# Listing the copies of a finished value product one slot later, behind an exponential, in a bucketed attention with a gated FFN

## The chip, the core and the metric

The kernel runs on one core of a Trainium2 chip. The engines of the core are TensorE (PE in the profile, with its weight loads apart as PEld), VectorE (DVE), ScalarE (ACT), GpSimd (POOL) and SyncE (SP, which only issues transfers here). Each engine takes its own list of instructions in order; an instruction waits on semaphores for what it needs of other engines. The metric is the device time of one execution in microseconds, lower being better.

## The reference

The first half is attention in which a query sees only the keys of its own hash bucket: six signs of a projection of q and of k make the bucket, and scores of other buckets are masked.

```python
mask = q_bucket[:, :, :, None] == k_bucket[:, :, None, :]
scores = scale * np.matmul(q, k.transpose(0, 1, 3, 2))
scores = np.where(mask, scores, -1000000000.0)
scores = scores - np.max(scores, axis=-1, keepdims=True)
attn = np.exp(scores)
attn = attn / (np.sum(attn, axis=-1, keepdims=True) + 1e-09)
x = np.matmul(attn, v)
```

The heads' outputs are then set side by side (512 channels) and go through a gated FFN: a causal convolution with 5 taps over the sequence gives a gate, sigmoid of it is multiplied with `x @ w_val`, and the product goes through `w_out`. Batch 4, 8 heads, sequence 768, head size 64, all in fp32.

## The kernel before

A **unit** is one head of one batch (32 units, numbered from 0). Its 768 queries are cut into 6 **tiles** of 128, so there are 192 tiles. One pass of the main loop (line 541) is a **slot**: slot k writes down, for several tiles at once, the steps at different stages. The order in which the Python code writes them down is the order of each engine's list (`manual_schedule`, line 522); no planner moves them.

In slot k the list is, in this order:

- ACT copies the transposed probabilities of tile k-4 out of PSUM (`keep_transposed`, line 369, two copies). With the last tile of a unit, the unit's value product is put into the list `avs`.
- DVE takes the row maxima of tile k (line 317), then the scale and the bias of its exponential (lines 323 and 327). In even slots the row sums and reciprocals of two earlier tiles stand between (lines 341 and 346).
- POOL multiplies tile k-2 by its reciprocals (`normalise`, line 351).
- PE makes the scores of tile k+1 (line 311, four matmuls). They go into one of two PSUM buffers named s, so tile k+1 reuses the buffer of tile k-1.
- ACT makes the exponential of tile k (line 335), which reads the scores and the bias.
- `convs` is stepped (line 569), in odd slots only while k is under 60 and in every slot from 60 on. A step of `pair_x` first splits the pair's outputs into a high part (two casts on DVE, line 403) and a low part (two subtractions on POOL, line 404), and in later steps makes the convolution's five taps (lines 412 and 414).
- `moes`, the FFN's matmuls of the batch before, is stepped: four matmuls a step (lines 445 and 470), with their products and splits on DVE and POOL (lines 450, 454 and 456) and the output copies (lines 476 and 478). In some slots no step, in a few three.
- preparation of the next unit, and other small lists.
- in odd slots `avs` is stepped twice (lines 583 and 584). One step of `attn_v` is two matmuls into the PSUM tile av, one for each half of the queries; six steps make a unit's value product.
- PE transposes tile k-3 (line 360, six transposes into two PSUM buffers named tp).

A unit's last tile comes to `keep_transposed` in a slot with k mod 6 = 3. The value product's six steps stand in the slots with k mod 6 = 3, 5 and 1. In the kernel before, the sixth step, at the end of the slot with k mod 6 = 1, also writes down what follows the matmuls: for the first unit of a pair (an even unit) the memset of a new tile x on POOL (line 387), then two copies of av into x on ACT (line 391), and for the second unit of a pair (an odd unit) the entry of `pair_x` into `convs` (line 395). PSUM tile av has one buffer, so the next unit's value product needs these copies done.

Of the kernel before, what the change touches and what calls it, by code (L numbers as in the profile page):

```python
# [26 lines left out]
def kernel(  # L27
# [109 lines left out]
    def load_conv():  # L137
        if conv_w.dtype == mybir.dt.int64:
            w = const.tile([P, NP * KW, 2], I32, name="cw64")
            nc.sync.dma_start(out=w, in_=conv_w.bitcast(I32).rearrange("p (n t) -> p n t", t=2))  # L140
            t = const.tile([P, NP * KW], FP32, name="cwt")
            yield
            a, d = yield from from_float64(w, t)
            yield
            nc.vector.tensor_tensor(out=cw_sb, in0=d, in1=a, op=ALU.add)
        else:
            nc.sync.dma_start(out=cw_sb, in_=conv_w)

    def load_weights():
        parts = [(src[:, c, :], hl[0][:, c, :], hl[1][:, c, :])  # L150
                 for src, hl in ((w_val, wv), (w_out, wo)) for c in range(NP)]
        here = []

        def fetch():
            if len(here) == len(parts):
                return
            src = parts[len(here)][0]
            if src.dtype == mybir.dt.int64:
                w = wst.tile([P, 512, 2], I32, name="w64")
                nc.sync.dma_start(out=w, in_=src.bitcast(I32).rearrange("p (n t) -> p n t", t=2))  # L160
            else:
                w = wst.tile([P, 512], FP32, name="w32")
                nc.sync.dma_start(out=w, in_=src)
            here.append(w)

        fetch()
        for n, (_, hi, lo) in enumerate(parts):
            yield
            yield from split_weight(here[n], hi, lo, fetch)

    def load_raw(i):
        if i < len(units):
            b, h = units[i]
            raws[i] = raw.tile([P, S], FP32, name="r")
            nc.sync.dma_start(out=raws[i], in_=qk[b, h])

    def load_values(i):
        b, h = units[i]
        if h % 2 == 0:
            vts[i] = vp.tile([P, KB, P], FP32, name="vt")  # L180
            nc.sync.dma_start(out=vts[i], in_=v[b, h // 2])
        else:
            vts[i] = vts[i - 1]
# [145 lines left out]
    def exponentials(k):  # L329
        s, nb = ss.pop(k), nbs.pop(k)  # L330
        p = pp.tile([P, 2, HS], FP32, name="p")
        if k % 2 == 0:
            cur["sm"] = small.tile([P, 2, 2], FP32, name="sm")
        sm = cur["sm"]
        nc.scalar.activation(out=p, in_=s[:, :, 0:HS], func=AF.Exp, bias=nb, scale=gs.pop(k), accum_out=sm[:, k % 2, 0:1])  # L335
        ps[k] = (p.rearrange("p a b -> p (a b)"), sm)
# [12 lines left out]
    def normalise(k):  # L349
        p, _ = ps[k]  # L350
        nc.gpsimd.tensor_scalar(out=p, in0=p, scalar1=rcs.pop(k), scalar2=1.0, op0=ALU.mult, op1=ALU.mult)  # L351
# [22 lines left out]
    def attn_v(i, pts):  # L374
        b, h = units[i]
        hh, c = h % 2, h // 2
        av = ps_v.tile([P, 512], FP32, name="av")
        vt = vts[i]
        for kb in range(KB):
            if kb:  # L380
                yield
            for s, pt in enumerate(pts):
                nc.tensor.matmul(out=av[s * D:(s + 1) * D, 0:HS], lhsT=vt[:, kb, hh * D:(hh + 1) * D], rhs=pt[kb // 3][:, kb % 3, :],  # L383
                                 start=(kb == 0), stop=(kb == KB - 1), tile_position=(0, s * D))
        if hh == 0:
            x = cur["x"] = xp.tile([P, S + KW - 1], FP32, name="x")
            nc.gpsimd.memset(x[:, 0:KW - 1], 0.0)
        x = cur["x"]
        for s in range(2):
            o = KW - 1 + s * HS  # L390
            nc.scalar.copy(out=x[hh * D:(hh + 1) * D, o:o + HS], in_=av[s * D:(s + 1) * D, 0:HS])  # L391
        if hh == 1:
            if c == 0:
                cur["xs"], cur["g"] = {}, []
            convs.append(pair_x(b, c, x, cur["g"], cur["xs"]))

    def pair_x(b, c, x, gs, xs_):
        for o in (0, HS):
            xh = xs.tile([P, HS], FP32R, name="xh")
            xl = xs.tile([P, HS], FP32R, name="xl")  # L400
            xs_[(c, o)] = (xh, xl)
            x0 = x[:, KW - 1 + o:KW - 1 + o + HS]
            nc.vector.tensor_copy(out=xh, in_=x0)  # L403
            nc.gpsimd.tensor_tensor(out=xl, in0=x0, in1=xh.bitcast(FP32), op=ALU.subtract)  # L404
        yield
        g = gp.tile([P, S], FP32, name="g")
        gs.append(g)
        for k in range(KW):
            yield
            w = cw_sb[:, c * KW + k:c * KW + k + 1]  # L410
            if k == 0:
                nc.gpsimd.tensor_scalar(out=g, in0=x[:, 0:S], scalar1=w, scalar2=1.0, op0=ALU.mult, op1=ALU.mult)  # L412
            else:
                nc.vector.scalar_tensor_tensor(out=g, in0=x[:, k:k + S], scalar=w, in1=g, op0=ALU.mult, op1=ALU.add)  # L414
        if c == NP - 1:
            yield
            for g in gs:
                nc.scalar.activation(out=g, in_=g, func=AF.Sigmoid)
            cur["gates"] = 2
            moes.append(moe(b, xs_, gs))  # L420
# [84 lines left out]
    avs, convs, moes, us = [], [], [], {}  # L505
    accs = [(ps_m, "m")]

    def step(gens):

        while gens:  # L510
            try:
                return next(gens[0])
            except StopIteration:
                gens.pop(0)
# [7 lines left out]
    with tc.manual_schedule(engines=ENGINES):  # L522
        for i in range(5):
            load_raw(i)
        load_values(0)
        rest = first_prep()
        next(rest)
        weights = [[load_weights()], [load_conv()]]
        preps = [first_bits(), prep(1)]
        scores(0)  # L530
        next(preps[1])
        step(preps)
        step(weights[0])
        step(weights[1])
        ahead = [early_bits()]
        near = {i: [bits(i)] for i in (4, 8, 12)}
        marks = {10: near[4], 11: ahead, 16: near[4], 17: ahead, 22: ahead, 28: ahead, 34: near[8], 40: near[8], 46: ahead, 52: ahead,
                 54: ahead, 56: ahead, 58: near[12], 60: near[12], 62: ahead, 64: ahead}
        for gens in near.values():
            step(gens)  # L540
        for k in range(N + LAG + 1):
            if 0 <= k - LAG - 1:
                keep_transposed(k - LAG - 1)
            pair = k % 2 == 0 and 0 <= k - 2 < N
            if k < N:
                maxima(k)
            if pair:
                row_sums(k - 2)
            if k < N:
                factors(k)  # L550
            if pair:
                recip(k - 2)
            if 0 <= k - 2 < N:
                normalise(k - 2)
            if k < N:
                shifts(k)
            if k == 0:
                finish([rest])
            if k + 1 < N:
                if tiles[k + 1][0] != tiles[k][0]:  # L560
                    finish(preps)
                    preps = [prep(tiles[k + 1][0] + 1)]
                scores(k + 1)
            if k < N:
                exponentials(k)
            if k - 1 in marks and k - 1 not in (11, 17):
                step(marks[k - 1])
            if k >= 60 or k % 2:
                step(convs)

            thin = k // 6 % 8 in (7, 0) and k < 186
            for _ in range(3 if cur["gates"] else (1, 0)[k % 2] if thin else 1):
                step(moes)
            cur["gates"] = max(0, cur["gates"] - 1)
            step(preps)
            if k in marks:
                step(marks[k])
            if k in (3, 7, 9, 13, 15):
                step(weights[1])
            if k % 6 != 3 and k > 4:  # L580
                step(weights[0])
            if k % 2:
                step(avs)
                step(avs)
            if 0 <= k - LAG < N:
                transposes(k - LAG)
        accs[:] = [(ps_m, "m"), (ps_t, "tp"), (ps_s, "s"), (ps_t, "tp"), (ps_s, "s")]
        finish(avs)
        cur["gates"] = 0
        cur["end"] = True  # L590
        while convs:
            step(convs)
            step(moes)
        finish(moes)
# [59 lines left out]
```

## Time and profile before

| what | us |
|---|---|
| median of 3 runs | 614.88 |
| lowest and highest | 613.47, 615.2 |
| the profiled execution, its own time | 613.79 |
| span of the profiled execution | 611.9 |
| TensorE busy | 585.5 |
| VectorE busy | 428.8 |
| ScalarE busy | 420.2 |
| GpSimd busy | 386.5 |

The span is the stretch of the profiled execution from the first instruction to the last. Busy time is the union of an engine's instructions. A row of instructions in order of time gives start and length in us, engine, line, operation, output and inputs, and in brackets the time that the engine stood idle before it with what ended that idle time. A row of a group gives the total of its busy time, the mean length in ns, and the idle time before it. In the chain of waits each piece is the work that the next piece waited for. TensorE's instructions are pipelined, so neighbouring rows can overlap by some hundredths to tenths of a microsecond.

### The profile page before, as it was taken

Reading aid. Unit: us, or ns where it says so; the run is one execution under the profiler, and the core shown is the slowest. Engines: PE = TensorE matmul, PEld = TensorE weight load, DVE = VectorE, ACT = ScalarE, POOL = GpSimd, SP = SyncE. Lnnn points to the kernel's source line nnn. Section 1 sums busy time; section 2 is a strip of 40 time slices with the busy share of each in tenths; the row PEclk is TensorE's granted clock in tenths of the full one; section 3 lists DMA queues with packets and bytes.
Section 4 is the critical chain, followed back from the end, with each engine's and each line's share of the span. In section 5 each row is a group of like instructions: output and inputs, shape, how many; then the busy total and the mean of one; then the engine's idle time right before and its main releaser. Section 6 shows DMA issues by size and latency. Waiting matters only on the chain.

```text
span 611.9 us, 10670 instructions
## 1 busy us (share of the span) xinstructions
PE 585.5 (96%) x3496; PEld 422.1 (69%) x3496; DVE 428.8 (70%) x1020; ACT 420.2 (69%) x881; POOL 386.5 (63%) x373
## 2 busy tenths in 40 slices
PE   5889999999999999999999999999999999999997
PEld 2656665665567777776667777777768787775995
DVE  6788889898776856587657857578765867565532
ACT  2778888787787766677796767677787676764300
POOL 3566877878656766677655768477745776454321
PEclk9999999999999999999999999999999999999999
DMA  7476566455742342233334323423333123100111
GB/s 231 123 206 198 161 175 177 131 160 148 226 109 81 83 121 70 82 105 86 111 90 123 80 74 89 113 83 92 101 87 90 45 55 100 47 19 1 51 52 51
DMA packets 29030, 64.64 MB, mean 106 GB/s; under 512 B 4936, under 2 KB 10056, under 8 KB 28976
## 3 DMA queue, kind: packets, MB, share of 16 engines
q1 hardware_dynamic: 28832, 63.93, 38.1%
q8 instruction: 28, 0.46, 0.3%
q14 instruction: 26, 0.21, 0.1%
q10 hardware_dynamic: 144, 0.03, 0.0%
HBM read 30.60 MB, written 7.86 MB: 63 GB/s over the span
## 4 chain that ended last, share of the span: by engine, by line
PE 80%; ACT 15%; DVE 3%; issue 1%; DMA 1%; ACTq 0%; DVEq 0%
PE av L383 22%; PE s L311 20%; PE tp L360 16%; PE m L470 8%; PE m L445 7%; ACT p L335 6%; ACT pt L369 5%; ACT x L391 3%; PE m L217 2%; PE tp L445 1%; PE tp L470 1%; PE s L470 1%; PE s L445 1%; DVE nm L317 1%; DMA packed<-in_proj_dram 1%
## 5 line engine op out<-in xcount | busy, mean ns | idle before, releaser
L351 POOL TENSOR_SCALAR p<-p,ri 128x768 f32<-128x768 f32 x192 | 205.4, 1074 | 152.1 <-DVE nb L327 130.9
L317 DVE TENSOR_REDUCE nm<-s 128x1 f32<-128x768 f32 x192 | 182.8, 952 | 72.1 <-PE s L311 71.3
L369 ACT COPY pt<-tp 128x384 f32<-128x384 f32 x384 | 165.9, 485 | 86.0 <-PE tp L360 85.3
L335 ACT ACTIVATE p<-s,nb,gs 128x768 f32<-128x768 f32 x192 | 193.0, 1005 | 29.6 <-DVE nb L327 26.9
L360 PEld LDWEIGHTS tp<-ident,p 128*128 128x128 f32 x1152 | 129.5, 142 | 75.4 <-issue 50.1
L360 PE MATMUL tp<-ident,p 128*128 128x128 f32 x1152 | 164.7, 279 | 2.6 <-ACT pt L369 1.6
L383 PE MATMUL av<-pt,vt 128*64 128x384 f32 x768 | 144.9, 498 | 0.0
L311 PE MATMUL s<-ak,aq 76*128 76x384 f32 x384 | 117.9, 388 | 14.6 <-ACT p L335 12.6
L311 PE MATMUL s<-bk,bq 128*128 128x384 f32 x384 | 101.7, 346 | 0.3 <-DVE bq L285 0.3
L383 PEld LDWEIGHTS av<-pt,vt 128*64 128x64 f32 x768 | 47.0, 136 | 60.5 <-issue 60.4
L311 PEld LDWEIGHTS s<-ak,aq 76*128 76x128 f32 x384 | 59.2, 194 | 28.8 <-ACT p L335 25.2
L414 DVE SCALAR_TENSOR_TENSOR g<-x,cw_sb,g 128x768 f32<-128x768 f32 x64 | 75.9, 1187 | 2.2 <-POOL g L412 2.1
L311 PEld LDWEIGHTS s<-bk,bq 128*128 128x128 f32 x384 | 71.5, 193 | 1.1 <-DVE bq L285 0.8
L456 POOL TENSOR_TENSOR hl<-ht,hh 128x384 fp32r<-128x384 f32 x32 | 32.3, 1009 | 40.0 <-DVE hh L454 40.0
L200 POOL TENSOR_TENSOR bq<-r,aq 128x768 fp32r<-128x768 f32 x31 | 56.8, 1833 | 0.1
L391 ACT COPY x<-av 64x384 f32<-64x384 f32 x64 | 30.4, 475 | 32.1 <-PE av L383 31.5
L404 POOL TENSOR_TENSOR xl<-x,xh 128x384 fp32r<-128x384 f32 x32 | 33.4, 1057 | 17.0 <-DVE xh L403 17.0
L327 DVE TENSOR_SCALAR nb<-nm,gs 128x1 f32<-128x1 f32 x192 | 40.6, 211 | 3.5
L445 PE MATMUL m<-xh,wv 128*128 128x384 f32 x200 | 42.8, 338 | 0.0
L450 DVE TENSOR_TENSOR ht<-m,g 128x384 f32<-128x384 f32 x25 | 13.9, 556 | 37.9 <-PE m L445 33.4
L335 ACT ACTIVATION_READ_ACCUMULATOR p<-s,nb,gs 128x1 f32 x192 | 39.5, 206 | 0.0
L470 PE MATMUL m<-wo,hh 128*128 128x512 f32 x144 | 38.1, 394 | 0.0
(86 smaller groups left out, 477.9 us busy)
## 6 DMA issues: line engine op xcount, KB each, us to landing
r<-in_qk_dram SPq DMA_DIRECT2D x32, 384.0 KB
vt<-in_v_dram SPq DMA_DIRECT2D x16, 384.0 KB
out_dram<-o SPq DMA_DIRECT2D x24, 256.0 KB
ak<-aq SPq DMA_DIRECT2D x31, 192.0 KB
bk<-aq SPq DMA_DIRECT2D x31, 192.0 KB
bk<-bq SPq DMA_DIRECT2D x31, 192.0 KB
bq<-aq SPq DMA_DIRECT2D x31, 192.0 KB
hh<-in_qk_dram SPq DMA_DIRECT2D x16, 192.0 KB
```

The costliest lines, as they stand in the source:

```text
L200: nc.gpsimd.tensor_tensor(out=bq, in0=r, in1=aq.bitcast(FP32), op=ALU.subtract)
L311: nc.tensor.matmul(out=s[:, hf, 0:HS], lhsT=lq[0:n, qs], rhs=rk[0:n, hf * HS:(hf + 1) * HS], start=n == M, stop=n == P)
L317: nc.vector.tensor_reduce(out=nm, in_=s[:, :, 0:HS], axis=AX.XY, op=ALU.max, negate=True)
L335: nc.scalar.activation(out=p, in_=s[:, :, 0:HS], func=AF.Exp, bias=nb, scale=gs.pop(k), accum_out=sm[:, k % 2, 0:1])
L351: nc.gpsimd.tensor_scalar(out=p, in0=p, scalar1=rcs.pop(k), scalar2=1.0, op0=ALU.mult, op1=ALU.mult)
L360: nc.tensor.transpose(out=tp[:, n * P:(n + 1) * P], in_=p[:, kb * P:(kb + 1) * P], identity=ident)
L369: nc.scalar.copy(out=pt[:, :, qo:qo + P], in_=tp[:, 0:HS].rearrange("p (a b) -> p a b", b=P))
L383: nc.tensor.matmul(out=av[s * D:(s + 1) * D, 0:HS], lhsT=vt[:, kb, hh * D:(hh + 1) * D], rhs=pt[kb // 3][:, kb % 3, :], start=(kb == 0), s ...
L391: nc.scalar.copy(out=x[hh * D:(hh + 1) * D, o:o + HS], in_=av[s * D:(s + 1) * D, 0:HS])
L414: nc.vector.scalar_tensor_tensor(out=g, in0=x[:, k:k + S], scalar=w, in1=g, op0=ALU.mult, op1=ALU.add)
L445: nc.tensor.matmul(out=acc[:, 0:HS], lhsT=wv[wi][:, c, j * P:(j + 1) * P], rhs=xs_[(c, o)][xi], start=(m == 0), stop=(m == 11))
L470: nc.tensor.matmul(out=acc, lhsT=hs[(o, j)][hi][:, tb * P:(tb + 1) * P], rhs=wo[wi][:, j, :], start=(m == 0), stop=(m == 11))
```

## The change

A `yield` is put between the value product's last matmuls and what follows them, so the sixth step ends with the matmuls. In the slots with k mod 6 = 2 one more step of `avs` is written down, directly behind that slot's exponential and ahead of the step of `convs`; it holds the memset, the two copies and the entry into `convs`. Since the entry is made in the slot with k mod 6 = 2 ahead of the step of `convs`, from slot 60 on the first step of `pair_x` stays in that slot, where it is in the kernel before. On ACT the two copies of line 391 now stand behind the two transposed copies of tile k-4 and the exponential of tile k of that slot, instead of ahead of them.

```diff
@@ attn_v
             for s, pt in enumerate(pts):
                 nc.tensor.matmul(out=av[s * D:(s + 1) * D, 0:HS], lhsT=vt[:, kb, hh * D:(hh + 1) * D], rhs=pt[kb // 3][:, kb % 3, :],
                                  start=(kb == 0), stop=(kb == KB - 1), tile_position=(0, s * D))
+        yield
         if hh == 0:
             x = cur["x"] = xp.tile([P, S + KW - 1], FP32, name="x")
             nc.gpsimd.memset(x[:, 0:KW - 1], 0.0)
@@ the main loop
             if k < N:
                 exponentials(k)
+            if k % 6 == 2:
+                step(avs)
             if k - 1 in marks and k - 1 not in (11, 17):
                 step(marks[k - 1])
             if k >= 60 or k % 2:
                 step(convs)
```

## The prediction

> **What bounds the kernel now.** I read the page first, then the waits, the chain in a thin early stretch, and then the instructions in order of time around the copies.
>
> ```profile
> span 611.9 us, 10670 instructions
> PE 585.5 (96%) x3496; PEld 422.1 (69%) x3496; DVE 428.8 (70%) x1020; ACT 420.2 (69%) x881; POOL 386.5 (63%) x373
> PE 80%; ACT 15%; DVE 3%; issue 1%; DMA 1%; ACTq 0%; DVEq 0%
> ...
> L335 ACT ACTIVATE p<-s,nb,gs 128x768 f32<-128x768 f32 x192 | 193.0, 1005 | 29.6 <-DVE nb L327 26.9 <-DVE cw L97 0.8 <-POOL p L351 0.6
> ...
> L391 ACT COPY x<-av 64x384 f32<-64x384 f32 x64 | 30.4, 475 | 32.1 <-PE av L383 31.5
> ...
> PE s L311 <- ACT p L335: 12.6, 31, 1.5
> ```
>
> TensorE (PE) is busy 96% of the span and carries 80% of the chain: it sets the end, and a change counts only where it moves a stall of PE. Its largest one is line 311 (scores) waiting for line 335 (exponential): 12.6 us in 31 waits. The two score buffers explain it: the scores of tile n+2 need the buffer that the exponential of tile n has read. The copies of line 391 keep ScalarE (ACT) busy 30.4 us, and ACT stands idle 31.5 us before them because they are listed right behind the value matmuls that they read.
>
> I write c for the slot with c mod 6 = 1 in which a unit's value product ends, and t for the time from the start of its first copy today. Here is unit 4 (instructions in order of time, then a piece of the chain; columns: start, length, what).
>
> ```profile
> 107.83 0.44 PE L360 MATMUL tp<-ident,p 128*128 128x128 f32 x2
> ...
> 107.94 0.96 ACT L391 COPY x<-av 64x384 f32<-64x384 f32 x2 [0.74 <-PE av L383]
> 108.93 0.86 ACT L369 COPY pt<-tp 128x384 f32<-128x384 f32 x2
> 109.67 1.01 ACT L335 ACTIVATE p<-s,nb,gs 128x768 f32<-128x768 f32 x1
> ...
> 110.83 0.98 PE s L311 x4
> ```
>
> After the value product PE waits through copies (0.96), transposed copies (0.86) and exponential c+1 (1.01) before the scores of tile c+3 start at 110.83: t=2.89. This chain is what the change cuts.
>
> **The change part by part: no new work.** No instruction is added or removed except that the small memset of a new x (POOL, 0.1 us) is listed one slot later, behind a normalisation; nothing reads those four columns before the convolution, so I put it at zero. Two copies of 0.47 to 0.48 us move on ACT past two transposed copies and one exponential. No DMA moves, and SP's queue keeps its order.
>
> **Where ACT's own order gains.** Without the copies, ACT's next work is the transposed copies of tile c-3, which wait for transposes that PE starts right behind the value product. Three places, from slots of units 4, 10 and 23:
>
> ```profile
> 103.01 0.87 PE L360 MATMUL tp<-ident,p 128*128 128x128 f32 x6
> 103.59 0.86 ACT L369 COPY pt<-tp 128x384 f32<-128x384 f32 x2 [0.50 <-PE tp L360]
> 103.64 0.59 PE L311 MATMUL s<-ak,aq 76*128 76x384 f32 x2
> ...
> 210.61 0.82 PE L360 MATMUL tp<-ident,p 128*128 128x128 f32 x6
> 211.50 0.62 PE L311 MATMUL s<-ak,aq 76*128 76x384 f32 x2
> ...
> 434.32 0.86 ACT L369 COPY pt<-tp 128x384 f32<-128x384 f32 x2
> 434.94 0.85 PE L360 MATMUL tp<-ident,p 128*128 128x128 f32 x6
> 437.12 1.51 PE L383 MATMUL av<-pt,vt 128*64 128x384 f32 x8
> ```
>
> ACT's copy starts 0.58 us after the transposes that it waits for (103.01 to 103.59). In unit 4 they start at t=-0.11 (107.83), so the transposed copies could start at t=0.47, exponential c+1 at 0.47+0.74=1.21 (0.74 is 108.93 to 109.67) instead of 1.73, and PE's scores c+3 0.52 us sooner. But the copies then stand at 1.21+0.98=2.19 (today the next copies start 0.98 behind an exponential) and end at 3.15. The transposed copies of tile c-2, the last that the next value product needs, start behind them at 3.18 and give their first half about 0.48 later, at 3.66; PE reads such a half some 0.14 us on (434.32 plus 0.48, to 434.94), at 3.79. The product's first matmul, 0.18 us of it (1.44 in eight), needs nothing of this, so it runs as if started at 3.61. Today it starts at 3.80 (437.12 less the unit's 433.32, whose row stands below): **0.18 us** a thin unit, not 0.52. The rest of the wait is moved, not removed.
>
> With gated-FFN matmuls between, less was stalled. The rows at 210.61 and 211.50 (unit 10) put the scores 0.89 behind the transposes, where six unstalled transposes pass in 0.63 (103.01 to 103.64): gain 0.27 with the rounding. Where the four filler matmuls are the 512-wide ones the scores are not late (0.65): gain 0. The other units are read in the same way. Those without the conflict below: units 0 to 6 give 1.0 together (in three of them the bias of exponential c+1 is ready only at t=1.2, which leaves 0.08), units 7 and 8 0.07 each, 10 and 12 0.27 each, 14 0.13, 18 0.26, 22 0.18, 16 and 24 0.15 each (there the next table load and sigmoids on ACT end later by as much as the copies moved), 20, 26 and 28 nothing. Sum **2.5 us**. Bounds: 0 (all absorbed by VectorE's lateness) to about 5 (0.2 for each of 25 units, the 31 waits of 12.6 us above not being exceeded).
>
> **What then waits: VectorE.** The copies of an odd unit complete a pair, and its split (line 403, two casts on VectorE, DVE) is stepped in slot c+1, directly behind the place to which the copies move. From slot 60 on it is stepped in every slot, so in the eleven odd units 9 to 29 the casts stay in slot c+1, ahead of the maxima of tile c+2, while their input comes 2.19 us later. DVE takes its instructions in order: behind the waiting cast stand the FFN's DVE work and the maxima, and behind those exponential c+2 and PE's scores c+4. In slots under 60 the split is stepped in odd slots only, two slots later in time, and the wait is nothing. Unit 9, then unit 23:
>
> ```profile
> 191.13 0.98 ACT L391 COPY x<-av 64x384 f32<-64x384 f32 x2 [1.21 <-PE av L383]
> 191.64 1.68 DVE L403 CAST xh<-x 128x384 fp32r<-128x384 f32 x2 [0.95 <-ACT x L391]
> 192.09 1.02 POOL L404 TENSOR_TENSOR xl<-x,xh 128x384 fp32r<-128x384 f32 x1 [0.46 <-DVE xh L403]
> 193.25 0.94 DVE L317 TENSOR_REDUCE nm<-s 128x1 f32<-128x768 f32 x1
> ...
> 197.71 0.59 PE L311 MATMUL s<-ak,aq 76*128 76x384 f32 x2
> ...
> 433.32 0.97 ACT L391 COPY x<-av 64x384 f32<-64x384 f32 x2 [1.33 <-PE av L383]
> 435.05 1.15 DVE L454 CAST hh<-ht 128x384 fp32r<-128x384 f32 x1
> 436.12 0.94 DVE L317 TENSOR_REDUCE nm<-s 128x1 f32<-128x768 f32 x1
> 437.60 0.99 ACT L335 ACTIVATE p<-s,nb,gs 128x768 f32<-128x768 f32 x1 [0.69 <-DVE nb L327]
> 439.19 0.60 PE L311 MATMUL s<-ak,aq 76*128 76x384 f32 x2
> ```
>
> Even now DVE waits 0.95 us for the copy in unit 9, and in unit 23 the exponential waits 0.69 us for the bias: this path has no slack to give. Worked from t: in unit 9 the casts begin at 0.51 and the maxima at 2.12. Both go 2.19 later: maxima at 4.31. From the maxima to the exponential's possible start it is 1.48 (436.12 to 437.60), from there to the scores that reuse its buffer 1.16 (109.67 to 110.83). So scores c+4 can start at 4.31+1.48+1.16=6.95 at the earliest (I use 6.92, with the maxima at 2.10 as in units 11 and 15). Today they start at 197.71: t=6.58. Loss 0.35. The same 6.92 against each unit's own start, and 0.28 more where one cast (hh, line 454) stands between, uncontended at 0.35 less overlap: 7.20.
>
> ```profile
> 226.97 0.97 ACT L391 COPY x<-av 64x384 f32<-64x384 f32 x2 [1.40 <-PE av L383]
> 233.78 0.43 PE L311 MATMUL s<-ak,aq 76*128 76x384 f32 x1
> ...
> 401.87 0.97 ACT L391 COPY x<-av 64x384 f32<-64x384 f32 x2 [0.64 <-PE av L383]
> 404.07 0.56 DVE L450 TENSOR_TENSOR ht<-m,g 128x384 f32<-128x384 f32 x1 [0.83 <-PE m L445]
> 407.75 0.59 PE L311 MATMUL s<-ak,aq 76*128 76x384 f32 x2
> ...
> 262.02 0.87 PE L360 MATMUL tp<-ident,p 128*128 128x128 f32 x6
> 268.25 0.59 PE L311 MATMUL s<-ak,aq 76*128 76x384 f32 x2
> ...
> 294.19 0.97 ACT L391 COPY x<-av 64x384 f32<-64x384 f32 x2 [1.56 <-PE av L383]
> 300.07 0.59 PE L311 MATMUL s<-ak,aq 76*128 76x384 f32 x2
> ```
>
> Unit 11 starts them at t=6.81: +0.12. Unit 15, with none of the FFN's matmuls there, at 5.88 (300.07-294.19): +1.04. With hh between: units 17, 25, 29 (as unit 9, 6.57) +0.63 each, units 19 and 27 (as unit 11) +0.40 each, unit 23 (439.19-433.32=5.87) +1.33, unit 13 +1.09 (its copies start late today, so its t counts from 0.12 behind the transposes at 262.02: 6.11). Unit 21 has a product of 0.56 us (line 450) between, so 7.43 against 5.88: +1.56. Sum **8.2 us**. These are lateness on PE against today, so the earlier gain in the same units is already spent in them. Behind the late scores nothing else becomes the end: POOL's normalisation of tile c goes about 2 us later, but its transposes come over 7 us after the copies, and unit 15's extra ACT copy of an output (line 478) delays the value product by less than the 1.04.
>
> **The price that before cannot show** is the second cast of a pair. In unit 9 the two casts take 1.68 us, because the second runs beside POOL's subtraction (192.09) and ends only after it; the group's lengths are:
>
> ```profile
> L403 DVE CAST xh<-x x32: 349/360/1182, 64.5 to 566.6; 128x384 fp32r<-128x384 f32 x32
> ```
>
> Shortest 349 ns, longest 1182. The second cast begins when the second copy has landed, POOL's subtraction when the first cast has: 192.09 against about 192.14, a lead of 0.05 for POOL. After the change both follow copies at the same spacing and POOL stands idle, so I take 1182; at 349 the casts end 0.83 sooner. The Trainium skill, "SBUF — State Buffer", section "Who interferes with whom", says that a DVE cast in its two-port mode and a GpSimd instruction hold a shared port pair as an exclusive lock, and whichever issues first makes the other wait its whole length. The trace agrees (1182 against 349 ns); by that rule the loss hangs on which of the two issues first, and it is the second rival here if DVE does.
>
> **The sum:** PE runs the units one behind the other, so what each gains or loses adds up. The profiled execution took 613.8 us, of them 611.9 span; 613.8 - 2.5 + 8.2 = 619.5 us. That execution lies 1.1 below the median of the timed runs, 614.88, from which the same step gives 620.6. I forecast **620.0**, with 617.5 to 622.5 as its own range.
>
> **The rivals.** (1) *Slower still* (chance 0.13): POOL's second subtraction also catches hh, which then takes 1.15 as at 435.05 instead of 0.35. That is 0.8 more in the seven units with hh: 8.2+5.6-2.5, or 625.1. Against it: hh stands directly behind the cast, and POOL waits for that cast's end. (2) *The second cast issues ahead of POOL* (0.12): scores c+4 possible at 6.10, with hh 6.38, with the product 6.6. Units 9, 17, 25 and 29 then gain 0.2 to 0.27, 13, 15, 21 and 23 lose 0.27, 0.4, 0.74 and 0.51, the others nothing: +1.1-2.5, or 612.4. For it speaks only that the lead is 0.05 us. (3) *Faster* (0.07): exponential c+2 is not late, since DVE reaches the maxima as early as today; it decides where the copies land before DVE comes to the cast. Then odd units gain as even ones do, 1.7 in all: 609.6. The 0.95 us idle before the cast at 191.64 speaks against it. (4) *Nothing to be seen* (0.06): ACT's gains and DVE's waits both vanish in slack, 613.8 to 614.9; the 96% of PE speaks against slack.
>
> **How the numbers follow.** The forecast's own case has 0.62. A measurement of this kernel tells a difference from 0.3%, 1.8 us, about 613.0 to 616.7. Slower: the forecast and the first rival, 0.75. Within: the fourth and half of the second, 0.12. Faster: the third and the other half, 0.13. The range leaves out the third rival, half of the second and half of the first, 0.19: 613.0 to 624.5.
>
> **What would show it.** In the changed profile ACT's idle time before the copies (31.5) falls to near nothing and shows before the transposed copies; PE's scores c+3 come about 0.5 sooner in thin units while the next value product comes only about 0.2 sooner. In units 9 to 29 the casts of line 403 start about t=2.7 with a wait for line 391 that was 10.7 us in five cases and becomes 15 to 25 in eleven, and line 311 waits for line 335 in slot c+3, 0.1 to 1.6 us, with the bias (line 327) late before it. I am wrong if casts wait and scores c+4 do not, if the second casts run 0.36 us, or if units 0 to 6 do not get shorter.

## The result, and the profile after

The changed kernel takes 624.96 us (median of 5 runs, 624.32 to 625.85) against 614.04 us before in the same comparison: a ratio of 1.0174, with a 95% interval of 1.0163 to 1.0185. It is slower by 10.9 us. The forecast was 620.0, slower by about 6, with a range from 613.0 to 624.5, and the measured time lies above it.

The page of the changed kernel, and its waits, in the parts that answer to those shown of before (the lines behind 385 have moved by one, so the copies are line 392, the casts of a split 404, hh 455):

```profile
span 622.9 us, 10683 instructions
PE 591.3 (95%) x3496; PEld 427.9 (69%) x3496; DVE 431.1 (69%) x1020; ACT 419.6 (67%) x881; POOL 389.0 (62%) x373
PE 62%; DVE 17%; ACT 17%; issue 1%; DMA 1%; POOL 0%; ACTq 0%; POOLq 0%; DVEq 0%
...
L335 ACT ACTIVATE p<-s,nb,gs 128x768 f32<-128x768 f32 x192 | 192.4, 1002 | 45.9 <-DVE nb L327 44.4
...
ACT p L335 <- DVE nb L327: 44.4, 39, 6.1
...
DVE xh L404 <- ACT x L392: 36.6, 12, 6.4
...
PE s L311 <- ACT p L335: 19.3, 39, 1.5
...
ACT x L392 <- PE av L383: 3.8, 1, 3.8
```

Of the kernel before, the row of waits that answers to the casts' is:

```profile
DVE xh L403 <- ACT x L391: 10.7, 5, 6.3
```

The wait that the change was to act on is gone: ACT stood idle 31.5 us before the copies and now 3.8. But the chain now runs 17% of the span over VectorE, where it was 3%, and three waits that follow one from the other have grown: casts for copies from 10.7 to 36.6 us (30.2 of them in the eleven odd units 9 to 29, where the prediction had said 15 to 25), exponentials for their bias from 26.9 to 44.4, scores for exponentials from 12.6 to 19.3. Here is unit 23, first VectorE, then ScalarE, then TensorE, each in order of time (hh is the cast of the FFN's product, line 455):

```profile
443.94 0.86 DVE L404 CAST xh<-x 128x384 fp32r<-128x384 f32 x2 [2.36 <-ACT x L392]
444.72 1.16 DVE L455 CAST hh<-ht 128x384 fp32r<-128x384 f32 x1
445.80 0.94 DVE L317 TENSOR_REDUCE nm<-s 128x1 f32<-128x768 f32 x1
...
442.31 1.01 ACT L335 ACTIVATE p<-s,nb,gs 128x768 f32<-128x768 f32 x1
...
443.44 0.97 ACT L392 COPY x<-av 64x384 f32<-64x384 f32 x2
444.43 0.86 ACT L369 COPY pt<-tp 128x384 f32<-128x384 f32 x2
447.28 0.99 ACT L335 ACTIVATE p<-s,nb,gs 128x768 f32<-128x768 f32 x1 [1.98 <-DVE nb L327]
...
444.46 2.01 PE L383 MATMUL av<-pt,vt 128*64 128x384 f32 x8
446.40 0.87 PE L360 MATMUL tp<-ident,p 128*128 128x128 f32 x6
448.41 0.62 PE L311 MATMUL s<-ak,aq 76*128 76x384 f32 x2 [1.14 <-ACT p L335]
```

VectorE waits 2.36 us for the copy; the maxima behind the casts come 2 us late, the exponential waits 1.98 us for the bias, and TensorE 1.14 us for the exponential. This is the path that the prediction described.

Since TensorE runs the units one behind the other, the time between the ends of two successive value products, after less before, shows where the 11.1 us up to the last unit came from (sums over the two traces):

```
                                        predicted   measured
up to unit 0's value product                 -        +0.32
intervals behind units 0 to 6              -1.0       +0.42
interval behind unit 7                     -0.07      +0.61
intervals behind odd units 9 to 29         +8.2       +9.59
  of them: u9 0.50, u11 0.29, u13 1.21, u15 1.11, u17 0.75, u19 0.55,
           u21 1.65, u23 1.47, u25 0.75, u27 0.53, u29 0.78
the other intervals                        -1.5       +0.14
sum                                        +5.7      +11.08
```

The loss is where it was expected, 1.4 us larger; the gain that was to pay for a third of it did not come. Units 0 to 6 did not get shorter, which the prediction had named as a sign of being wrong.

### The profile page after: what moved, and what is told of

It reads as the page before. It is cut to its first block, busy times and chain, and to the rows that moved or that the text cites. A ratio compares the mean times of both kernels' runs of the same rounds, so it can differ in the third digit from the quotient of the medians.

```text
span 622.9 us, 10683 instructions
## 1 busy us (share of the span) xinstructions
PE 591.3 (95%) x3496; PEld 427.9 (69%) x3496; DVE 431.1 (69%) x1020; ACT 419.6 (67%) x881; POOL 389.0 (62%) x373
## 4 chain that ended last, share of the span: by engine, by line
PE 62%; DVE 17%; ACT 17%; issue 1%; DMA 1%; POOL 0%; ACTq 0%; POOLq 0%; DVEq 0%
PE av L383 17%; PE s L311 15%; PE tp L360 13%; ACT p L335 8%; DVE nm L317 6%; PE m L446 5%; PE m L471 5%; ACT pt L369 4%; DVE g L415 4%; ACT x L392 2%; DVE xh L404 2%; PE m L217 2%; ACT g L419 1%; PE tp L446 1%; DVE nb L327 1%
## 5 line engine op out<-in xcount | busy, mean ns | idle before, releaser
L335 ACT ACTIVATE p<-s,nb,gs 128x768 f32<-128x768 f32 x192 | 192.4, 1002 | 45.9 <-DVE nb L327 44.4
L383 PE MATMUL av<-pt,vt 128*64 128x384 f32 x768 | 151.4, 499 | 0.4 <-ACT x L392 0.3
L311 PE MATMUL s<-ak,aq 76*128 76x384 f32 x384 | 117.9, 388 | 21.2 <-ACT p L335 19.3
L383 PEld LDWEIGHTS av<-pt,vt 128*64 128x64 f32 x768 | 52.2, 136 | 62.4 <-issue 50.8
L415 DVE SCALAR_TENSOR_TENSOR g<-x,cw_sb,g 128x768 f32<-128x768 f32 x64 | 79.4, 1240 | 2.5 <-POOL g L413 2.1
L404 DVE CAST xh<-x 128x384 fp32r<-128x384 f32 x32 | 21.0, 663 | 38.4 <-ACT x L392 36.6
L446 PEld LDWEIGHTS m<-xh,wv 128*128 128x128 f32 x200 | 35.3, 188 | 0.3 <-DVE ht L451 0.2
```

Source lines behind the costliest of these rows:

```text
L311: nc.tensor.matmul(out=s[:, hf, 0:HS], lhsT=lq[0:n, qs], rhs=rk[0:n, hf * HS:(hf + 1) * HS], start=n == M, stop=n == P)
L446: nc.tensor.matmul(out=acc[:, 0:HS], lhsT=wv[wi][:, c, j * P:(j + 1) * P], rhs=xs_[(c, o)][xi], start=(m == 0), stop=(m == 11))
```

## The experiments

**Casts a slot later.** The step of `pair_x` is written ahead of the copies' new place, so from slot 60 on a pair's casts stand behind the next tile's maxima and bias. ACT's order stays as in the changed kernel.

```diff
-            if k % 6 == 2:
-                step(avs)
             if k - 1 in marks and k - 1 not in (11, 17):
                 step(marks[k - 1])
             if k >= 60 or k % 2:
                 step(convs)
+            if k % 6 == 2:
+                step(avs)
```

> The changed kernel, but the step of the pair split is written ahead of the copies' new place, so that from slot 60 on the two casts of a pair stand one slot later, behind the next tile's maxima and bias. ACT's order stays that of the changed kernel. Theory A (VectorE held by the waiting casts): the eleven odd units 9 to 29, which lose 9.6 us in the changed kernel's trace, and the 1.2 us that follow in units 16 and 22, come back: 625.0 - 10.8 = 614.2, between 613 and 616. Theory B (the copies' place on ACT itself, ahead of the transposed copies that the next value product needs, makes the loss): 622 or more.

Measured: 611.94 us, ratio to before 0.9961 (0.9949 to 0.9974). Its waits:

```profile
ACT p L335 <- DVE nb L327: 16.9, 16, 6.1
PE s L311 <- ACT p L335: 10.6, 28, 1.5
DVE xh L404 <- ACT x L392: 4.1, 1, 4.1
```

The casts no longer wait, and all three waits are shorter than before the change. The copies stand on ACT where the changed kernel has them, so their place there is not what costs; what costs is the cast waiting for them at the head of VectorE's list. The kernel came out 2.3 us below what theory A expected, and below its range of 613 to 616, which the control further down explains in part.

**Odd units alone, and even units alone.** The edit is shown for the odd units; the other kernel has `hh == 0` in its place.

```diff
-        yield
+        if hh == 1:
+            yield
         if hh == 0:
```

> The change for odd units alone (the second of each pair); even units keep their copies where they are in the kernel before. Theory A: the eleven odd units lose their 9.6 us and units 16 and 22 the 1.2 that DVE is late behind them, the early odd units up to 0.8: 614.0 + 11 = 625, between 623 and 626.5. Theory B (each unit loses about 0.35 by ACT's order): half of the loss, about 619.5.

> The change for even units alone. By the prediction's terms a gain of about 2 us (612). By the trace of the changed kernel (thin units gain nothing since the value product's two halves run side by side and both end 1.4 us after the later one's data; two or three units with FFN matmuls gain 0.3): within 1 us of the kernel before, 613.2 to 614.8. Theory B: half of the loss, about 619.5.

Measured: odd units alone 624.8 us, ratio 1.0173 (1.0157 to 1.0189), the whole loss; even units alone 613.16 us, ratio 0.9986 (0.9977 to 0.9995), at the lower end of its expected 613.2 to 614.8. The eleven intervals behind odd units lose 9.70 us in the first and 0.02 in the second. Theory B, a price that every unit pays on ACT, falls: it had put both kernels at about 619.5.

**Subtractions later.** The two subtractions of a split on POOL stand in the pair's next step, behind a normalisation and other listed work.

```diff
             nc.vector.tensor_copy(out=xh, in_=x0)
-            nc.gpsimd.tensor_tensor(out=xl, in0=x0, in1=xh.bitcast(FP32), op=ALU.subtract)
         yield
+        for o in (0, HS):
+            xh, xl = xs_[(c, o)]
+            x0 = x[:, KW - 1 + o:KW - 1 + o + HS]
+            nc.gpsimd.tensor_tensor(out=xl, in0=x0, in1=xh.bitcast(FP32), op=ALU.subtract)
         g = gp.tile([P, S], FP32, name="g")
```

> The changed kernel, but the two subtractions on POOL of a pair's split stand in the next step of the pair instead of between and behind the two casts. If the second cast (or the cast behind it) is held because POOL's subtraction runs beside it, it takes 0.36 instead of 1.18 us, the maxima come 0.8 us sooner in all eleven odd units, and of their 9.6 us loss some 6 to 8 go: 616 to 619. If the length of that cast has another cause: 624 to 626, with second casts of 1.18 still.

Measured: 621.38 us, ratio 1.0121 (1.0106 to 1.0136); the expectation of 616 to 619 was too high a gain. The trace shows why it is half. Unit 17 first in the changed kernel:

```profile
338.30 1.67 DVE L404 CAST xh<-x 128x384 fp32r<-128x384 f32 x2 [2.43 <-ACT x L392]
339.90 0.35 DVE L455 CAST hh<-ht 128x384 fp32r<-128x384 f32 x1
340.17 0.95 DVE L317 TENSOR_REDUCE nm<-s 128x1 f32<-128x768 f32 x1
...
342.78 0.62 PE L311 MATMUL s<-ak,aq 76*128 76x384 f32 x2 [0.85 <-ACT p L335]
```

and with the subtractions later (VectorE, then POOL; then unit 9, VectorE and POOL):

```profile
338.72 0.86 DVE L404 CAST xh<-x 128x384 fp32r<-128x384 f32 x2 [2.44 <-ACT x L392]
339.50 0.35 DVE L458 CAST hh<-ht 128x384 fp32r<-128x384 f32 x1
339.76 0.95 DVE L317 TENSOR_REDUCE nm<-s 128x1 f32<-128x768 f32 x1
...
339.93 1.00 POOL L460 TENSOR_TENSOR hl<-ht,hh 128x384 fp32r<-128x384 f32 x1 [2.72 <-DVE hh L458]
340.91 0.91 POOL L351 TENSOR_SCALAR p<-p,ri 128x768 f32<-128x768 f32 x1
341.78 1.98 POOL L409 TENSOR_TENSOR xl<-x,xh 128x384 fp32r<-128x384 f32 x2
...
195.68 1.68 DVE L404 CAST xh<-x 128x384 fp32r<-128x384 f32 x2 [3.32 <-ACT x L392]
...
196.12 1.02 POOL L409 TENSOR_TENSOR xl<-x,xh 128x384 fp32r<-128x384 f32 x1 [1.95 <-DVE xh L404]
```

In unit 17 POOL's list has the FFN's subtraction (hl, line 460) first, which waits for a later cast; so no POOL instruction runs beside the two casts, they take 0.86 instead of 1.67 us, and the interval behind the unit loses nothing (-0.05, against +0.75). The casts are as short in all seven units that have hh there: together these lose 4.9 us less. Of that 1.5 us is lost again elsewhere, most of it behind units 14, 18 and 26, where VectorE now comes to the maxima of tile c+1 0.3 to 0.5 us later than in the changed kernel. In units 9, 11, 15 and 21 POOL has nothing else in front, starts its subtraction the moment the first cast is done, just as before, and the second cast is held. So the hold costs 0.8 us where it falls, and the prediction took it rightly; but listing the subtraction later does not make it later on an idle engine.

**The value product's two halves in the other order.** Each step's matmul of the second 384 queries is written ahead of that of the first.

```diff
-            for s, pt in enumerate(pts):
+            for s, pt in reversed(list(enumerate(pts))):
```

> The changed kernel with the two halves of each step of the value product in the other order, the second half's matmul ahead of the first half's. If the product lasts 1.4 us from the arrival of the second half's data in either order, because both halves run side by side: 624.3 to 625.7, the thin units' next transposes again 5.2 us behind the value product. If the first half's matmuls give a head start, as the prediction had it: about 0.2 to 0.4 us lost in each of some fifteen units, 628 to 631.

Measured: 624.15 us, ratio 1.0159 (1.0146 to 1.0173): no slower than the changed kernel. It lies 0.15 below the expected 624.3 to 625.7; in the traces 0.5 us of its lead over the changed kernel stands at a load that is treated further down. The value product behind unit 4 and the transposes behind it, before the change, changed, and swapped:

```profile
111.73 1.51 PE L383 MATMUL av<-pt,vt 128*64 128x384 f32 x8
113.18 0.88 PE L360 MATMUL tp<-ident,p 128*128 128x128 f32 x6
```

```profile
110.89 0.62 PE L311 MATMUL s<-ak,aq 76*128 76x384 f32 x2 [0.24 <-ACT p L335]
...
111.80 1.94 PE L383 MATMUL av<-pt,vt 128*64 128x384 f32 x8
113.67 0.87 PE L360 MATMUL tp<-ident,p 128*128 128x128 f32 x6
```

```profile
112.33 1.51 PE L383 MATMUL av<-pt,vt 128*64 128x384 f32 x8 [0.37 <-ACT pt L369]
113.77 0.87 PE L360 MATMUL tp<-ident,p 128*128 128x128 f32 x6
```

In the changed kernel the product starts as soon as the scores are done, but lasts 1.94 us; with the halves swapped it starts 0.37 us late and lasts 1.51. In both the transposes begin about 5.19 us behind the end of the value product before (113.67 less 108.48; 113.77 less 108.57); before the change it was 5.28 (113.18 less 107.89). The two halves run side by side in different columns of the array (`tile_position`): in the swapped product and in that of before, their matmuls start in pairs within 0.01 us. So the half whose data are there early gains nothing by starting alone. In either order the transposes begin 1.4 us after the later half's first matmul, which starts at 112.24 in the changed kernel and at 112.33 in the swapped one.

**The casts a slot later without moving the copies** (a control of the first experiment), and **the copies of even units moved from slot 60 on alone**:

```diff
-            if k >= 60 or k % 2:
+            if (k >= 60 or k % 2) and not (k >= 60 and k % 12 == 8):
                 step(convs)
```

> The kernel before with the pair split alone one slot later from slot 60 on; the copies stay. If split_next's gain comes from the copies' new place (scores c+3 no longer behind them, 0.3 us in each of a dozen units): no gain here, 613.3 to 614.9. If it comes from the later casts themselves: 612 or less.

```diff
-        yield
+        if hh == 0 and cur["k"] >= 60:
+            yield
```

> Copies moved for even units from slot 60 on alone, so no cast waits for them and nothing ahead of slot 60 changes. By even_only's trace (0.3 us each in units 10, 12, 18, 24 by rows of the intervals that follow, 0.1 to 0.2 in three more, and 1.0 lost at the late load of r, which should be gone): 614.1 - 1.4 = 612.7, between 612 and 613.3. If the load of r is late all the same: 613.7.

Measured: 613.28 us for the control, ratio 0.9982 (0.9973 to 0.9991), just below its expected 613.3 to 614.9; and 613.44 us for the even units, ratio 0.9973 (0.9949 to 0.9997; 0.998 by the two medians, 613.44 and 614.43), 0.1 above its own range. The control's trace gains 0.75 and 0.73 us in the two intervals behind units 16 and 24 and loses 0.5 in two others: part of the first experiment's gain, about 0.2% of 0.4%, is the later casts by themselves. In the even-unit kernel the units 10, 12, 18 gain the 0.3 us that the prediction gave them, and unit 14 loses 0.66, because a tap of the convolution on VectorE took 1.72 instead of 1.01 us there and the bias came late; whether that is more than chance was not tried.

**Both parts from slot 60 on.** Copies moved in slots from 60 on alone, casts a slot later by the edit of the first experiment (not repeated here); then the same with the subtractions later as well, and the first of these once more beside it.

```diff
+            cur["k"] = k
...
-        yield
+        if cur["k"] >= 60:
+            yield
```

> Copies moved from slot 60 on alone, and there the pair split one slot later, as in split_next. If the parts add up, it keeps split_next's gain behind slot 60 and drops what its trace lost ahead of it (0.5 us in units 0 to 6, 1.4 us where a load of r was issued 5 us later): 611.9 - 1.9 = 610.0, between 609.3 and 611. If the late load of r is chance or comes in spite of it: 611 to 612.

> from60_split_next with the two subtractions of a split in the pair's next step, so that POOL's subtraction does not run beside the second cast wherever POOL has other work listed first. If the 0.4 to 0.6 us that from60_split_next still loses in units 15, 20, 22, 23 and 28 come of casts held by POOL, up to 2 us less: 609 to 610.5. If they come of the casts' place in VectorE's list alone, or the hold only moves to other instructions: 610.5 to 612.

> The same kernel as from60_split_next once more, beside the new version on the same chip: 610.3 to 611.8.

Measured: 611.04 us, ratio 0.9946 (0.9933 to 0.9958), and 610.92, 0.9946 (0.9932 to 0.9959), in the repetition; with later subtractions 611.13, 0.9958 (0.9944 to 0.9971), no better. The first is the fastest kernel of the study, 3 us below the one before, though 1 us above the 610.0 that was expected of it and just outside the range to 611. The chain of its page:

```profile
span 608.3 us, 10692 instructions
PE 83%; ACT 11%; DVE 3%; issue 1%; DMA 1%; POOL 0%; ACTq 0%; DVEq 0%; POOLq 0%
```

So in this kernel the copies behind the exponential are worth having from slot 60 on, as long as nothing on VectorE waits for them in front of the maxima. Of the 0.54%, the control has 0.18% by the later casts alone. Ahead of slot 60 the move does not pay: with it units 0 to 6 lose 0.4 us in the first experiment, without it nothing.

**A load that the change moved.** The interval behind unit 7 lost 0.61 us, and 0.79, 1.05 and 1.37 in three of the experiments (subtractions later, even units alone, casts later). There TensorE multiplies four tiles r for the buckets (line 217). Before the change, in the changed kernel, and with the casts later, SyncE's issue of the last of these loads and the products:

```profile
153.23 0.62 SPq L175 DMA_DIRECT2D r<-in_qk_dram  x1
161.38 0.85 PE L217 MATMUL m<-r,proj_sb 128*32 128x384 f32 x8
```

```profile
157.93 0.58 SPq L175 DMA_DIRECT2D r<-in_qk_dram  x1
162.21 1.38 PE L217 MATMUL m<-r,proj_sb 128*32 128x384 f32 x8
```

```profile
158.04 0.58 SPq L175 DMA_DIRECT2D r<-in_qk_dram  x1
162.14 0.85 PE L217 MATMUL m<-r,proj_sb 128*32 128x384 f32 x6
163.45 0.83 PE L217 MATMUL m<-r,proj_sb 128*32 128x384 f32 x2 [0.47 <-DMA r<-in_qk_dram]
```

SyncE's list is not written out by hand as the other four are, and an edit can change its order. In the changed kernel this load stands behind four transfers that it stood ahead of, goes out 4.7 us later, and the products last 1.38 instead of 0.85 us. In four kernels it goes out at about 158 us (the changed kernel, casts later, even units alone, subtractions later). There the products last 1.38 to 2.15 us, and the fourth waits for this very load (with the casts later, 0.47 us of idle TensorE in the row above). In the kernel before and the other seven it goes out at 152.8 to 154.6 us, the products last about 0.85 us, and they do not wait for it. What puts the load later in these four lists is not shown.

## Why the prediction was wrong in size

**What bounds the kernel, and the direction: right.** TensorE sets the end, the wait for ScalarE's copies moved instead of vanishing, and VectorE's in-order list turned it into late maxima, a late bias and late scores in the eleven odd units. The first three experiments show where it starts: odd units alone carry the loss, and moving only the casts takes it all away.

**The loss, 8.2 us: 9.59 measured.** The step that failed is "the copies then stand at 1.21+0.98". In even units they do; in odd units the copies start 1.13 us behind the exponential:

```profile
109.74 1.01 ACT L335 ACTIVATE p<-s,nb,gs 128x768 f32<-128x768 f32 x1
110.63 0.21 ACT L335 ACTIVATION_READ_ACCUMULATOR p<-s,nb,gs 128x1 f32 x1
110.72 0.95 ACT L392 COPY x<-av 64x384 f32<-64x384 f32 x2
```

This is even unit 4, 0.98 us from exponential to copies; in odd unit 23 above it is 442.31 to 443.44. In the eleven odd units it is 1.12 to 1.13 us, 0.14 more than the prediction had, which makes 1.5 us together where 1.4 is missing. Unit by unit the loss is 0.07 to 0.17 us above the forecast: 0.50 for 0.35, 0.29 for 0.12, 1.65 for 1.56, 1.47 for 1.33. The other terms of the path held: with t counted from the same point behind the value product, the scores of tile c+4 start at t=7.05 in units 9 and 11 (6.92 forecast) and at 7.31 in the units with hh (7.20 forecast).

**The held cast: right.** Where POOL stood idle the second cast was held in every odd unit, or the cast behind it (unit 23: 0.86 for two, then 1.16 for hh); the maxima came at the same time either way, t=4.70 in units 23 and 25.

**The gain, 2.5 us: a loss of 1.2 instead.** Three steps failed; they account for the 3.7 us between the two but for 0.3, by which the remaining units came out better than forecast.

First, the thin units 0 to 6, 1.4 us. "The product's first matmul needs nothing of this, so it runs as if started at 3.61" failed: the halves run side by side, and the start is worth nothing. The even units 2, 4 and 6 still gain 0.1 of the forecast 0.18, by luck: TensorE reads the half that it waits for 0.05 us after its copy (112.18 to 112.24 in unit 4), not 0.14. The odd units 1, 3 and 5 also pay the 0.14 us of their later copies. And behind units 3 and 5, two of the three that the prediction gave 0.08, VectorE reaches the maxima of tile c+1 0.2 us later, the exponential waits for its bias, and the moved copies stand behind it: they lose 0.35 each.

Second, "SP's queue keeps its order": it does not, and one late load cost 0.7 us against the forecast.

Third, 1.9 us: the units behind a stalled one were taken as undisturbed. Behind units 10, 14, 16 and 22 VectorE reaches the maxima of tile c+1 0.2 to 0.8 us later, counted from the end of the unit's value product. Here is unit 16, whose value product ends at 309.15 before and at 313.19 in the changed kernel (first before, then changed; in each VectorE, then ScalarE):

```profile
308.93 0.94 DVE L317 TENSOR_REDUCE nm<-s 128x1 f32<-128x768 f32 x1
310.93 1.01 ACT L335 ACTIVATE p<-s,nb,gs 128x768 f32<-128x768 f32 x1
```

```profile
313.76 0.94 DVE L317 TENSOR_REDUCE nm<-s 128x1 f32<-128x768 f32 x1
315.24 0.99 ACT L335 ACTIVATE p<-s,nb,gs 128x768 f32<-128x768 f32 x1 [0.67 <-DVE nb L327]
316.22 0.95 ACT L392 COPY x<-av 64x384 f32<-64x384 f32 x2
```

The maxima come 0.8 us later against that end, the exponential waits for its bias, and the moved copies stand behind the late exponential. The intervals behind units 16 and 22 lose 0.63 and 0.52 where 0.15 and 0.18 were to be gained; behind 10 and 14 it is -0.13 for -0.27 and +0.12 for -0.13. Both parts of the change are needed for this. With odd units moved alone VectorE is just as late in these four places, but the even units' copies stand ahead of the exponential, and the intervals lose only 0.24 behind 16, 0.08 behind 22 and nothing behind 10 and 14. With even units moved alone VectorE is in time, and the four gain 0.31, 0.06, 0.16 and 0.03. How the stall of an odd unit reaches these maxima, through the order of VectorE and POOL at the convolution's taps, is not worked out: in unit 16 the tap ahead of them starts 0.46 us later and lasts 2.15 instead of 1.81 us. Where neither applies the terms held: -0.27 behind unit 18 for -0.26, -0.33 behind 12 for -0.27.

**The rest, 0.3 us,** is the first transfer, which landed 0.4 us later in this execution, ahead of anything that the change touches.

**The rivals.** The first gave 625.1, next to what came, but by chance and by another mechanism: hh was not held on top of the casts (0.35 us at 339.90). The forecast's own range ended at 622.5, because the gain's lower bound was set at zero; that the units without the conflict could lose was in no rival.

## What to carry to other kernels

Moving an instruction later on its engine moves every reader of it later, and a reader that stands ahead of urgent work in another in-order list stalls that list: move the reader with it, past the urgent work, as the casts here. A matmul that waits in one half of the array's columns makes a step of two halves as late as its later half, so a head start for the other half is not a gain. Look at which lists are written out and which are planned: an edit that touches no transfer can still reorder transfers.

## What the runs showed that was not expected

- The copy of 64 rows out of PSUM into the upper half of a tile starts 1.11 to 1.13 us behind the exponential before it, the one into the lower half 0.98 to 0.99, in fifteen units of each kind: the latter starts while the accumulator is still being read (110.63 to 110.84 in unit 4), the former behind it. What makes the difference was not tried.
- The four products of line 217, side by side in columns, last 0.85 us when they start together. When the fourth starts late the group lasts longer by as much: 1.38 us when it starts 0.53 us behind its neighbours, 2.15 when it starts 1.3 us behind them.
- Two casts of a pair cost 0.62 to 0.86 us when POOL is elsewhere and 1.67 when its subtraction of 1.0 us starts between them. The hold can pass to the cast behind: in unit 23 it fell on hh, 1.16 instead of 0.35 us.
